# Row sums of two pieces of the exponentials: ScalarE's accumulator or one VectorE instruction, with a new order table

## The chip, the core and the metric

The kernel runs on one core of a Trainium2 chip. The metric is device time in microseconds: the median of three runs of the kernel before is 339.64 us (339.58 to 340.34).

The engines are TensorE (PE: matmuls; PEld are its weight loads), VectorE (DVE), ScalarE (ACT), GpSimd (POOL) and SyncE (SP, which here issues all DMAs). Each has a queue of its own and takes its instructions in order; an instruction whose inputs are not there holds up all that stand behind it on its engine.

## What is computed

Causal attention over 4 batches, 12 heads, 448 tokens and a head size of 64, and then a gated two-layer network with a spatial gate over the tokens:

```python
scores = scale * np.matmul(q, k.transpose(0, 1, 3, 2))
scores = np.where(mask, -1000000000.0, scores)          # mask: above the diagonal
scores = scores - np.max(scores, axis=-1, keepdims=True)
attn = np.exp(scores)
attn = attn / (np.sum(attn, axis=-1, keepdims=True) + 1e-09)
x = np.matmul(attn, v)                                  # then heads side by side: (4, 448, 768)
...
h = gelu(x @ w_in)                                      # 768 -> 1024, tanh form
u, v = (h[..., :d_ff // 2], h[..., d_ff // 2:])
v_n = (v - mu) / np.sqrt(var + 1e-06) * g_ln
v_s = np.einsum('ts,bsd->btd', w_sg, v_n) + b_sg[None, :, None]
return x + (u * v_s) @ w_out                            # 512 -> 768
```

The change touches the exponentials and their row sums.

## The kernel before

The work is cut into 24 pairs of heads (`pair`, six pairs a batch) and four networks (`mlp`, one a batch). No loop sets the order of execution: the functions only enter their steps in a list (`Order.add`, with the engine and with what a step reads and writes), and a table written out by hand, `ORDER`, says in which order the steps are issued. Each engine so gets its steps in the order of the table. A step is one instruction or a few; the table has 1915 of them. Places in a queue, where the text gives them, are counted from 0 in the steps of one engine.

A pair goes this way. SP loads `qk` (448 KB). TensorE makes the scores in two steps (`score`, L433) in four PSUM banks `s`; all PSUM tiles share eight banks. VectorE masks, scales and takes the row minimum of the negative scores in eight steps (`mxs`, L448; each with a read of an accumulator into `ngm`). Only the lower triangle is made; the rows of a head are cut into four chunks (`CH`), and the exponentials of a head into five pieces (`EX`): pieces 0, 2 and 3 have 128 rows and 448, 320 and 128 columns; pieces 1 and 4 have 64 rows and 64 columns. ScalarE makes each piece by one ACTIVATE (L456) into `P`, with an accumulator that adds up the row; its read is a second instruction, ACTIVATION_READ_ACCUMULATOR, which puts the sum in a place of `sm`. The `P` tiles of two heads lie side by side in one tile `PP`, with room for 2 x 1024 columns; there are three such tiles.

From `sm` the step `inv` on VectorE makes the total of each row (L466, TENSOR_REDUCE) and its inverse (L467); it reads all ten places of a pair. TensorE turns the inverses (L470, "the turn"), VectorE copies them (L471), and SP writes them to DRAM (L475) and reads them back spread over the partitions as `rb` (L478). Meanwhile `P` is transposed: for pairs 0 to 7 by TensorE (L500, `tx`, `ty`) and copied to `B` by ScalarE or VectorE (L505, L507), for pairs 8 to 23 by VectorE (L488) and four DMAs. TensorE multiplies with the values (`o`, L526), VectorE multiplies the result with `rb` (L553, `xt`), and `keep_x` splits it in two parts for the network.

The weights are loaded and split in the first 100 us or so beside the pairs: `win` (twelve loads of 512 KB), `wsg` (224 KB each) and `wout` (sixteen of 192 KB), each with a step on ScalarE (L368), two on VectorE (L370, an integer shift, and L372) and two on GpSimd. All matmuls of the networks are at L581; they are issued in steps of three (`group`). Seven matmuls on zeros (L341) stand near the start.

Of the kernel before, what the change touches and what calls it, by code (L numbers as in the profile page):

```python
# [44 lines left out]
PW = 1024  # L45
# [182 lines left out]
def attention_gated_mlp(ctx: ExitStack, tc: tile.TileContext, qk, vP, w_in, g_ln, w_sgT, b_sg, w_out, out):  # L228
# [60 lines left out]
    def act(n, fn, r, w, sb=False, extra=0, ring=()):  # L289
        od.add("act", (0.093 if sb else 0.051) + n / 1200 + 0.093 * extra, fn, r, w, ring=ring)  # L290

    def dve(n, fn, r, w, rate=1.0417, done=0.0, port=False, ring=()):
        od.add("dve", 0.068 + n * rate / 1000, fn, r, w, done, port=port, ring=ring)
# [474 lines left out]
```

## Time and profile before

| | |
|---|---|
| median of three runs | 339.64 us |
| the profiled execution | 341.12 us, of which 339.3 us are the span of the trace |
| TensorE busy | 326.6 us (96%) |
| VectorE busy | 258.3 us (76%) |
| ScalarE busy | 197.2 us (58%) |
| GpSimd busy | 174.1 us (51%) |
| DMA | 57.75 MB, 170 GB/s in the mean |

The profile is one execution. The busy share is a mean over the whole span and hides that the stretches have different limits; so the rows below are of stretches and of single instructions in order of time. In these the number in front is the start in microseconds, the second is the duration; neighbours on one engine overlap a little, so that the time that an instruction holds the queue is read from one start to the next. Idle time ahead of an instruction stands in brackets, with what ended it. "128x448 f32" is partitions by elements.

### The profile page before, as it was taken

To read this page: it belongs to the slowest core of one execution; us is meant where nothing else is said; L and a number is where in the kernel's file an instruction comes from. 1 tells how busy PE (TensorE), PEld (TensorE's weight loads), DVE (VectorE), ACT (ScalarE), POOL (GpSimd) and SP (SyncE) were. 2 spreads that over 40 slices of the span, in tenths; PEclk is the share of its full clock that TensorE was granted. 3 is DMA by queue.
4 is the path that set the end of the run, shared out by engine and by line. 5 is a ranking of instruction groups with operands and counts; after the bars stand their busy time and mean duration, and the time that the engine had idled before them with its cause. 6 is when DMAs were issued, how large, how long until landed. Compare 5 with 4: busy or idle time off the path is not lost.

```text
span 339.3 us, 7630 instructions
## 1 busy us (share of the span) xinstructions
PE 326.6 (96%) x2614; PEld 267.5 (79%) x2615; DVE 258.3 (76%) x762; ACT 197.2 (58%) x658; POOL 174.1 (51%) x225
## 2 busy tenths in 40 slices
PE   3999998999999999999999999999999999999994
PEld 2666675868988878878898878877988988889994
DVE  4899976999999988889699767798877521577512
ACT  3999987996667658476645727384645301344300
POOL 4457666787588843223236608402407833352670
PEclk9999999999999999999999999999999999999998
DMA  7887789592584889857769368557342651201003
GB/s 227 321 251 269 251 247 275 150 322 87 126 228 136 243 218 260 231 143 167 174 187 268 101 208 266 111 155 212 83 115 40 209 141 55 108 2 54 0 29 136
DMA packets 31255, 57.75 MB, mean 170 GB/s; under 512 B 3312, under 2 KB 15344, under 8 KB 31216
## 3 DMA queue, kind: packets, MB, share of 16 engines
q1 hardware_dynamic: 31216, 57.26, 58.1%
q8 instruction: 21, 0.34, 0.4%
q14 instruction: 18, 0.15, 0.2%
HBM read 33.39 MB, written 7.08 MB: 119 GB/s over the span
## 4 chain that ended last, share of the span: by engine, by line
PE 83%; ACT 6%; DVE 4%; DMA 4%; issue 1%; SPq 1%; DVEq 0%; ACTq 0%
PE m L581 63%; PE o L526 10%; PE s L433 8%; ACT P L456 5%; DMA rd<-rT 2%; DVE s L448 1%; DMA g<-in_w_out_dram 1%; DMA qk<-in_qk_dram 1%; ACT B L507 1%; ACT vn L368 1%; PE s L470 1%; DVE vn L372 1%; PE tx L500 1%; PE ty L500 1%; DVE vn L370 0%
## 5 line engine op out<-in xcount | busy, mean ns | idle before, releaser
L456 ACT ACTIVATE P<-s,ngm 64x64 f32<-64x64 f32 (+3 forms) x240 | 100.9, 434 | 35.3 <-DVE ngm L448 28.5
L448 DVE CUSTOM_DVE_ANT_0 s<-s,mask 128x192 f32<-128x192 f32 (+3 forms) x192 | 77.2, 438 | 11.2 <-PE s L433 10.0
L581 PE MATMUL m<-win,x 128*128 128x512 f32 (+1 forms) x264 | 65.7, 399 | 0.1
L581 PE MATMUL m<-x,win 128*128 128x448 f32 x288 | 61.5, 367 | 0.0
L581 PE MATMUL m<-g,wout 128*128 128x448 f32 x288 | 61.3, 368 | 0.0
L581 PEld LDWEIGHTS m<-x,win 128*128 128x128 f32 x288 | 53.7, 188 | 5.2
L581 PEld LDWEIGHTS m<-g,wout 128*128 128x128 f32 x288 | 53.5, 188 | 5.1 <-ACT P L456 0.2
L581 PEld LDWEIGHTS m<-win,x 128*128 128x128 f32 (+1 forms) x264 | 46.7, 183 | 11.9 <-POOL win L375 0.2
L433 PE MATMUL s<-qk 64*64 64x64 f32 (+5 forms) x768 | 46.6, 375 | 6.4 <-DMA qk<-in_qk_dram 5.1
L456 ACT ACTIVATION_READ_ACCUMULATOR P<-s,ngm 128x1 f32 (+1 forms) x240 | 49.9, 208 | 0.0
L433 PEld LDWEIGHTS s<-qk 64*64 64x64 f32 x768 | 30.4, 140 | 23.4 <-issue 10.1
L526 PE MATMUL o<-B,vraw 128*64 128x64 f32 (+4 forms) x672 | 45.3, 291 | 0.3 <-DVE B L505 0.3
L526 PEld LDWEIGHTS o<-B,vraw 128*64 128x64 f32 x672 | 33.0, 137 | 13.5 <-issue 5.5
L488 DVE STREAM_TRANSPOSE P<-P 128x1024 f32<-128x1024 f32 x32 | 38.9, 1228 | 2.1 <-DMA B<-P 1.8
L691 POOL TENSOR_TENSOR res<-x 128x448 f32<-128x448 f32 x24 | 27.6, 1166 | 21.5 <-DMA out_dram<-res 21.3
L581 PE MATMUL m<-wsg,vn 128*128 128x448 f32 x176 | 38.1, 367 | 0.0
L562 POOL TENSOR_TENSOR x<-xt,x 128x448 fp32r<-128x448 f32 x24 | 27.5, 1148 | 15.2 <-ACT x L561 14.9
L581 PEld LDWEIGHTS m<-wsg,vn 128*128 128x128 f32 x176 | 32.7, 188 | 2.9
L704 DVE TENSOR_TENSOR res<-m,res 128x448 f32<-128x448 f32 (+1 forms) x25 | 14.7, 600 | 19.0 <-PE m L581 19.0
L592 ACT ACTIVATE tmp<-tmp 128x448 f32<-128x448 f32 (+2 forms) x32 | 18.9, 601 | 16.4 <-DVE tmp L590 16.4
L625 POOL TENSOR_TENSOR mv<-mv,mhalf 128x1 f32<-128x1 f32 (+1 forms) x16 | 10.0, 626 | 35.8 <-DVE mv L623 35.7
L675 POOL TENSOR_TENSOR tmp<-tmp,g 128x448 f32<-128x448 f32 x16 | 18.3, 1148 | 17.5 <-DVE tmp L671 17.4
(77 smaller groups left out, 395.2 us busy)
## 6 DMA issues: line engine op xcount, KB each, us to landing
B<-P SPq DMA_DIRECT2D x64, 256.0 KB
qk<-in_qk_dram SPq DMA_DIRECT2D x24, 448.0 KB
vn<-in_w_in_dram SPq DMA_DIRECT2D x12, 512.0 KB
vraw<-in_vP_dram SPq DMA_DIRECT2D x24, 256.0 KB
rb<-rd SPq DMA_DIRECT2D x24, 224.0 KB
out_dram<-res SPq DMA_DIRECT2D x9, 448.0 KB
g<-in_w_out_dram SPq DMA_DIRECT2D x16, 192.0 KB
rd<-rT SPq DMA_DIRECT2D x48, 32.0 KB
```

Of the source, the lines that this page charges most:

```text
L433: nc.tensor.matmul(out=s[z][bk].t[64 * h:64 * h + 64, col:col + n], lhsT=qk_.t[r, 0, q0:q0 + 64], rhs=qk_.t[r, 1, k0:k0 + n], start=True, ...
L448: nc.vector.tensor_tensor_reduce(out=o, in0=i, in1=mk, scale=-0.125, scalar=3e38, op0=ALU.add, op1=ALU.min, accum_out=ngm[ib[z]][c][0:m])
L456: act(n, lambda c=c, m=m, k0=k0, n=n, bk=bk, col=col, off=off, kc=kc, i=i, z=z: nc.scalar.activation(out=P[i][0:m, off:off + n], in_=s[z][ ...
L488: dve(PW, lambda z=z: nc.vector.transpose(A[ia][:, :, :, z, :].rearrange("p g t k -> p t g k"), P[ib[z]]), Pk[z] + [kp], Ak, 1.105)
L526: nc.tensor.matmul(out=dst(o.t[r]), lhsT=vr.t[:, c, r], rhs=src(z), start=first and n == 0, stop=last and n == len(lst) - 1)
L562: pool_tt(S, lambda: nc.gpsimd.tensor_tensor(out=y.t[:, S + 64:], in0=x.t, in1=f(y.t)[:, 0:S], op=ALU.subtract), [x, y], [(y, 1)])
L581: nc.tensor.matmul(out=ps.t[0:l().shape[1], 0:n], lhsT=l(), rhs=rr(), start=(k == 0), stop=(k == len(mms) - 1))
L592: act(n, lambda: nc.scalar.activation(out=z(), in_=z(), func=AF.Tanh, scale=GS * GC), [], [t], True)
L625: od.add("pool", 0.46, lambda mv=mv, m=m: nc.gpsimd.tensor_tensor(out=mv.t[0:m, 1:2], in0=mv.t[0:m, 1:2], in1=mhalf[0:m], op=ALU.pow), ["s ...
L675: pool_tt(S, lambda z=z, u=u: nc.gpsimd.tensor_tensor(out=z(), in0=z(), in1=u.t, op=ALU.mult), [u], [t])
L691: pool_tt(S, lambda rr=rr, x=x, k=k: nc.gpsimd.tensor_tensor(out=rr.t[:, k, :], in0=f(x.t)[:, 0:S], in1=f(x.t)[:, S + 64:], op=ALU.add), [ ...
L704: dve(hi - lo, lambda rr=rr, ps=ps, z=z, lo=lo, hi=hi: nc.vector.tensor_tensor(out=rr.t[:, z, lo:hi], in0=ps.t[:, lo:hi], in1=rr.t[:, z, l ...
```

## The change

Pieces 1 and 4 are no longer summed by ScalarE: their ACTIVATE has no accumulator, and its read goes. One VectorE step a pair (`sums`) adds up the rows of these four pieces (two of each head) by one TENSOR_REDUCE over 64 partitions and 2 x 2 rows of 64 elements, and writes the four columns of `sm` that the reads had written. `inv` reads them as before. The table has 24 steps more (1939) and is another one from its start to its end: on TensorE 473 of 551 steps have another place, on VectorE 494 of 538, by up to 61. Nothing else is changed: tiles, buffers, the sizes of loads and what runs on which engine are the same.

```diff
@@ pair
             for z in range(2):
                 i = ib[z]
-                act(n, lambda c=c, ..., i=i, z=z: nc.scalar.activation(
+                own = k not in (1, 4)
+                act(n, lambda c=c, ..., i=i, z=z, own=own: nc.scalar.activation(
                     out=P[i][0:m, off:off + n], in_=s[z][bk].t[0:m, col + k0:col + k0 + n], func=AF.Exp,
-                    bias=ngm[i][c][0:m], scale=-1.0, accum_out=sm[ip][0:m, z, kc[0], kc[1]:kc[1] + 1]),
-                    [s[z][bk], ("ngm", i, c), kp, ks] + ([("P", i, k - 1)] if k == 1 else [("P", i, 2)] if k == 4 else []),
-                    [("P", i, k), ("sm", ip, z, k)], extra=2)
+                    bias=ngm[i][c][0:m], scale=-1.0,
+                    **({"accum_out": sm[ip][0:m, z, kc[0], kc[1]:kc[1] + 1]} if own else {})),
+                    [s[z][bk], ("ngm", i, c), kp] + [ks] * own + ([("P", i, k - 1)] if k == 1 else [("P", i, 2)] if k == 4 else []),
+                    [("P", i, k)] + [("sm", ip, z, k)] * own, extra=2 * own)
+        def sums():
+            t = PP[ib[0] // 2]
+            nc.vector.tensor_reduce(
+                out=sm[ip][0:64].rearrange("p z c t -> p z (c t)")[:, :, 7:10:2][:, :, ::-1],
+                in_=bass.AP(tensor=t.tensor, offset=t.offset + 384, ap=[[2 * PW, 64], [PW, 2], [384, 2], [1, 64]]),
+                op=ALU.add, axis=mybir.AxisListType.X)
+        dve(256, sums, [("P", i, k) for i in ib for k in (1, 4)] + [ks], [("sm", ip, z, k) for z in range(2) for k in (1, 4)])
```

The places that the two tables give to some steps (before, after):

| queue | step | before | after |
|---|---|---|---|
| SP | load of pair 1's `qk` | 2 | 1 |
| SP | load of pair 3's `qk` | 6 | 12 |
| SP | first and second load of `wout` | 17, 32 | 9, 19 |
| ScalarE | the ten exponentials of pair 0 | 1 to 10 | 0 to 10 |
| VectorE | `sums` of pair 0; `inv` of pair 0 | -; 16 | 18; 21 |
| VectorE | `inv` and L553 of pair 3 | 58, 83 | 62, 91 |
| VectorE | `inv` and L553 of pair 5 | 85, 106 | 89, 120 |
| VectorE | `inv` of pair 11 | 245 | 252 |
| TensorE | first scores of pair 3; turn of pair 11 | 22; 189 | 23; 186 |

Up to `inv` of pair 11 the new table has twelve `sums` more on VectorE, and four masks of pair 12 (two of 192 columns, two of 320) and one transpose of pair 11 (L488) less. Up to the turn of pair 11 it has five steps of three output matmuls less on TensorE and two such steps more.

## Rows read from the trace of the kernel before

**Rows 1.** Stretches of the span: microseconds, busy time and instructions of each engine, granted clock, DMA.

```profile
10.00:60.00 50.00, 46.73 (x485) 32.82 (x479) 42.85 (x174) 46.66 (x180) 31.67 (x37) 1.00 0.83 264
10.00:48.70 38.70, 36.73 (x398) 26.51 (x391) 34.32 (x134) 38.67 (x147) 24.00 (x29) 1.00 0.81 263
60.00:118.80 58.80, 58.80 (x477) 48.91 (x476) 57.12 (x168) 43.88 (x142) 47.40 (x64) 1.00 0.63 184
118.80:335.00 216.20, 216.20 (x1617) 182.80 (x1616) 152.58 (x395) 102.38 (x326) 91.02 (x98) 1.00 0.51 142
```

**Rows 2.** Chain that ended last, in order of time: start, microseconds, what.

```profile
15.73 2.39 ACT P L456 x12
...
281.17 53.88 PE m L581 x257
```

**Rows 3.** VectorE in order of time (start, duration, line, shapes), around pair 11's row sums.

```profile
115.05 0.39 DVE L448 CUSTOM_DVE_ANT_0 s<-s,mask 128x192 f32<-128x192 f32 x1
...
115.37 0.52 DVE L448 CUSTOM_DVE_ANT_0 s<-s,mask 128x320 f32<-128x320 f32 x1
...
115.82 0.53 DVE L448 CUSTOM_DVE_ANT_0 s<-s,mask 128x320 f32<-128x320 f32 x1
...
116.27 2.60 DVE L488 STREAM_TRANSPOSE P<-P 128x1024 f32<-128x1024 f32 x2
118.79 0.14 DVE L466 TENSOR_REDUCE tot<-sm 128x8 f32<-128x24 f32 x1
118.96 0.20 DVE L467 RECIPROCAL rs<-tot 128x8 f32<-128x8 f32 x1
```

**Rows 4.** TensorE in order of time: pair 3's scores, pair 8's scores, pair 11's turn.

```profile
20.25 1.16 PE L433 MATMUL s<-qk 64*64 64x448 f32 x12
...
55.84 0.98 PE L433 MATMUL s<-qk 64*64 64x448 f32 x10 [1.23 <-ACT P L456]
...
119.31 0.27 PE L470 MATMUL s<-ident,rs 128*8 128x128 f32 x1
```

**Rows 5.** Groups by line and shape: busy, mean ns of one, idle before.

```profile
L456 ACT ACTIVATION_READ_ACCUMULATOR P<-s,ngm 64x1 f32 x96 | 19.9, 208 | 0.0
...
L448 DVE CUSTOM_DVE_ANT_0 s<-s,mask 128x448 f32<-128x448 f32 x48 | 30.0, 634 | 0.6
...
L448 DVE CUSTOM_DVE_ANT_0 s<-s,mask 64x64 f32<-64x64 f32 x48 | 11.0, 236 | 8.1 <-PE s L433 8.1
...
L466 DVE TENSOR_REDUCE tot<-sm 128x8 f32<-128x24 f32 x24 | 3.9, 164 | 2.1 <-ACT P L456 2.1
```

**Rows 6.** ScalarE in order of time: a 64 by 64 exponential, its read, the next.

```profile
8.78 0.31 ACT L456 ACTIVATE P<-s,ngm 64x64 f32<-64x64 f32 x1
8.97 0.20 ACT L456 ACTIVATION_READ_ACCUMULATOR P<-s,ngm 64x1 f32 x1
9.07 0.31 ACT L456 ACTIVATE P<-s,ngm 64x64 f32<-64x64 f32 x1
```

**Rows 7.** VectorE in order of time: an integer shift of 512 elements.

```profile
8.50 0.41 DVE L370 TENSOR_SCALAR vn<-vn 128x512 int32<-128x512 int32 x1
```

**Rows 8.** VectorE in order of time: seven waits before 60 us, in brackets.

```profile
10.30 0.22 DVE L448 CUSTOM_DVE_ANT_0 s<-s,mask 64x64 f32<-64x64 f32 x1 [0.38 <-PE s L433]
...
11.76 0.37 DVE L448 CUSTOM_DVE_ANT_0 s<-s,mask 128x192 f32<-128x192 f32 x1 [0.26 <-PE s L433]
...
25.45 0.69 DVE L372 SCALAR_TENSOR_TENSOR vn<-vn 128x512 int32<-128x512 int32 x1 [0.57 <-ACT vn L368]
...
39.42 0.62 DVE L553 TENSOR_TENSOR xt<-o,rb 128x448 f32<-128x448 f32 x1 [0.41 <-DMA rb<-rd]
...
45.33 0.43 DVE L370 TENSOR_SCALAR g<-g 128x192 int32<-128x192 int32 x2 [1.38 <-DMA g<-in_w_out_dram]
...
54.12 0.62 DVE L553 TENSOR_TENSOR xt<-o,rb 128x448 f32<-128x448 f32 x1 [1.04 <-DMA rb<-rd]
...
57.01 0.23 DVE L448 CUSTOM_DVE_ANT_0 s<-s,mask 64x64 f32<-64x64 f32 x1 [1.62 <-PE s L433]
```

More of the change, by code (lines that the diff above doesn't have):

```diff
@@ L455, in pair @@
                 i = ib[z]
-                act(n, lambda c=c, m=m, k0=k0, n=n, bk=bk, col=col, off=off, kc=kc, i=i, z=z: nc.scalar.activation(
+                own = k not in (1, 4)
+                act(n, lambda c=c, m=m, k0=k0, n=n, bk=bk, col=col, off=off, kc=kc, i=i, z=z, own=own: nc.scalar.activation(
                     out=P[i][0:m, off:off + n], in_=s[z][bk].t[0:m, col + k0:col + k0 + n], func=AF.Exp,
-                    bias=ngm[i][c][0:m], scale=-1.0, accum_out=sm[ip][0:m, z, kc[0], kc[1]:kc[1] + 1]),
-                    [s[z][bk], ("ngm", i, c), kp, ks] + ([("P", i, k - 1)] if k == 1 else [("P", i, 2)] if k == 4 else []),
-                    [("P", i, k), ("sm", ip, z, k)], extra=2)
+                    bias=ngm[i][c][0:m], scale=-1.0,
[9 more added lines that the diff above has]
+        dve(256, sums, [("P", i, k) for i in ib for k in (1, 4)] + [ks], [("sm", ip, z, k) for z in range(2) for k in (1, 4)])
         sk = [("sm", ip, z, k) for z in range(2) for k in range(5)]
```

185 rows, old and new, of the table ORDER are left out of this document.

## The prediction

> **What bounds the kernel now.** I read the stretches of the span first [rows 1]: what matters is not the share of each engine but where TensorE stops. From 60 us to 335 us it is busy in every microsecond (58.80 of 58.80, then 216.20 of 216.20). Between 10 and 60 us it is busy for 46.73 of 50.00. So time can be won only where TensorE is still waiting for the others, in the first 60 us, or lost where they fall behind it later. The chain that ended last [rows 2] says the same: at first it runs over ScalarE's exponentials, and its last piece is 53.88 us of matmuls without a gap. What holds TensorE up at the start is first ScalarE: from 10 to 48.7 us it is busy 38.67 of 38.70 us [rows 1]. VectorE is next to it: idle 7.15 us between 10 and 60 us and only 1.68 us between 60 and 118.8 us. After 118.8 us VectorE has 63.6 us to spare in 216.2.
>
> The second thing to see is how close VectorE is to TensorE at the end of its dense stretch. Pair 11's row sums are added up (L466) at 118.79 us and inverted at 118.96 us, ready about 119.16 [rows 3]; TensorE turns them at 119.31 us [rows 4]. The slack is 0.15 us, although no wait is shown there. Up to that point the kernel is paced by VectorE's work plus VectorE's idle time: 1.68 + 7.15 = 8.8 us of it idle between 10 us and there. That sum is what I forecast with.
>
> **ScalarE's side: a relief.** Of 240 accumulator reads 96 go, those of the 64 by 64 pieces [rows 5]. The row of one says 208 ns, but a read overlaps its neighbours: an exponential starts at 8.78, its read at 8.97, the next exponential at 9.07 [rows 6]. The read holds the queue for 0.10 us, not 0.21. Four a pair are 0.4 us, the eight pairs that start before 60 us give 3.2 us, and all 24 give 9.6 us, of which those after the first ten pairs lie beside TensorE's unbroken work and are worth nothing. A piece's exponentials are also usable 0.1 us sooner.
>
> **VectorE's side: a load.** One TENSOR_REDUCE a pair over 2 x 2 x 64 = 256 elements of 64 partitions. No row of before has a long one. From the mask rows the slope of one element a partition is (634 - 236) / 384 = 1.04 ns, and the short reduce takes 164 ns for 24 elements, so its base is 139 ns and 256 elements take 404 ns [rows 5]. The next instruction starts about 0.07 us before the end of the one ahead (a mask step of 0.39 us at 115.05, with its read, is followed at 115.37 [rows 3]), so 0.33 us a pair; where L466 stands right behind it and needs its result there is no overlap (118.79, 0.14 long, then 118.96 [rows 3]): 0.44. From below: if it went at the rate of the integer shift (512 elements in 0.41 us [rows 7], less the base 0.53 ns an element), 256 elements would take 0.275 us, 0.21 with the overlap. I take 0.33, because the short reduce and the masks are the nearest rows in kind (one result an element, no doubling seen). In all 24 x 0.33 = 7.9 us; the twelve after pair 11 (4.0 us) are covered by the 63.6 us of idle VectorE, the twelve up to pair 11 (4.0 us) are not covered by anything but idle time.
>
> The Trainium skill has a rule here that speaks against the change. VectorE: DVE Perf Modes, in its rules for kernel authors and its tier table, says that `tensor_reduce` has only a program for one element a cycle, whatever the type, and advises against it on a hot path. By that rule the sum for twelve pairs is 4.0 us; by the shift's row it would be 2.5. No run here shows a long reduce yet.
>
> **The wait it adds.** The new instruction waits for two exponentials of each head, and everything behind it in VectorE's queue waits too, chiefly the next pair's masks, for which ScalarE in turn waits. In the new table the first stands at place 18 of VectorE's queue (counted from 0), behind six masks of pair 1, while the exponentials that it reads end at place 10 of ScalarE's: eleven short steps against seventeen, so ScalarE should be done first. For the later pairs L466 follows within two steps in 16 of 23 cases and within nine in the others, and L466 waited for all ten exponentials already; so I cost the wait at nothing, and if that cover is gone it is the idle time of the first rival.
>
> **The new order.** The table moves most instructions, by up to some 60 places on an engine. On the queues ahead of pair 11's reciprocals I compare what each engine has to do. VectorE: twelve sums more (+4.0), and four masks of pair 12 and one transpose of pair 11 are put behind it: 2 x 0.32 + 2 x 0.45 by their starts (115.05, 115.37, 115.82) and 1.15 of the two transposes' 2.60 [rows 3], so -2.7: net +1.3. TensorE: fifteen matmuls of the last phase go behind the turn and six come ahead of it, nine fewer at 53.88 / 257 = 0.21 us [rows 2]: it comes there 1.8 us sooner. So for the same end VectorE has to be there 1.3 + 1.8 - 0.15 = 3.0 us sooner in waiting: its idle time up to pair 11 has to fall from 8.8 to 5.8 us. What falls below that is gain, microsecond for microsecond, since TensorE runs without a gap behind it.
>
> Seven of these waits make 5.66 us [rows 8]; the rest, all under 0.5 us, I leave as they are. By the table:
> - two on pair 1's scores, 0.64 us: pair 1's load goes from third to second on SP's queue, ahead of 512 KB of weights. Gone.
> - 0.57 on ScalarE's weight step: that step has more room and ScalarE less to do. Gone.
> - 0.41 and 1.04 on the reciprocals that come back from DRAM: from a pair's L467 to its L553 there are 29 steps of VectorE instead of 25 (pair 3) and 31 instead of 21 (pair 5). 1.0 gone.
> - 1.38 on output weights: the first are loaded at places 9 and 19 of SP's queue, not 17 and 32, well ahead of VectorE's use. Gone.
> - 1.62 on pair 8's scores, which themselves waited 1.23 us for a bank that ScalarE's exponentials free [rows 4]: ScalarE has 3.2 us less to do by then. 1.2 gone.
>
> That is 4.8 of 5.66, with nothing new in their place: idle 8.8 - 4.8 = 4.0 us, and a gain of 4.8 - 3.0 = 1.8 us. SP's queue pays for it: pair 3's load stands behind 4992 KB, its own included, not 3328 (by the sizes in the code; six loads are pulled ahead of it), which at the pace of the first stretch (264 GB/s [rows 1]) is there about 19.4 us after the start instead of 12.9; TensorE took it up at 20.25 [rows 4] and does so one group of matmuls later now. One microsecond of margin; I cost it at nothing, else what it overruns. GpSimd's steps follow the weights and have no reader that is late.
>
> **How it stands to the time.** The profiled execution took 341.12 us (339.3 of span), 1.48 above the median of 339.64. 341.12 - 1.8 = 339.3 for such an execution, and 337.8 for the median.
>
> **Rivals.**
> 1. Slower: VectorE becomes the bound up to pair 11. ScalarE's relief is not used, because VectorE, with the sums and the same waits at other places, is late for the masks, and the exponentials wait for them (that ScalarE has to wait for masks soon after 48.7 us, when it is no longer full, speaks for it; that it has no wait of weight before [rows 1] speaks against). If the idle time stays at 8.8 us the price is the whole 3.0 us: 342.6. It decides from 5.8 us of idle up to pair 11.
> 2. No change: between 2.0 and 4.0 us of the waits go, the new load eats them, 338.6 to 340.6, middle 339.6. For it: VectorE is 86% busy in the first of these stretches and 97% in the second, and idle time that is closed at one place opens at another.
> 3. Faster by more: the reduce takes 0.21 us, or every one of the seven waits goes. 12 x 0.12 = 1.4 us gives 336.4; the waits 0.9, 336.9; both 335.5.
> 4. The change doesn't do what it says: the exponential without a read is as long as with it. Then ScalarE gains nothing, its 3.2 us stay, and 1.2 + 0.57 of the waits with it: 339.6, as rival 2.
>
> **How the numbers follow.** The forecast has 0.48 (336.9 to 338.6: gains of 2.7 to 1.0 us), rival 3 0.10, rivals 2 and 4 together 0.26, rival 1 0.16. A run of this kernel can tell some 0.3%, 1.0 us, from no change, so faster is below 338.6: 0.48 + 0.10 = 0.58; same 0.26; slower, above 340.7: 0.16. The range leaves out the far half of rival 3 and most of rival 1: 336.0 to 340.9.
>
> **What would show it.** Right: no read between 64 by 64 exponentials and starts 0.19 us apart; reduces of 64 x 256 of about 0.40 us; VectorE idle about 4 us between 10 us and pair 11's L466, and that row about 1.2 to 3.6 us earlier than 118.79, at the same or a little more VectorE work; TensorE without a gap behind it. Wrong: TensorE idle after 60 us, or waits of VectorE on `P` at the new line (the wait is real); a reduce of 0.28 us (rival 3); a late `qk` of pair 3 near 20 us; waits of TensorE on VectorE between 65 and 125 us (rival 1).

## The result, and the profile after

The changed kernel takes 342.88 us (median of four runs, 342.74 to 343.09), the kernel before beside it 339.99 (339.58 to 340.83). The ratio is 1.0082, with a 95% interval of 1.0060 to 1.0105: slower by 0.8%, where 337.8 us, a gain of 0.5%, was forecast. The profiled execution took 342.94 us with a span of 341.2, against 341.12 and 339.3 before; that execution of before had already lost 0.9 us at its start (last section), so by the profiles the loss is 1.8 us, and by the medians 2.9.

The stretches of the changed kernel (microseconds, then busy time and instructions of TensorE, its weight loads, VectorE, ScalarE and GpSimd, granted clock, DMA):

```profile
10.00:60.00 50.00, 44.67 (x484) 31.05 (x485) 46.47 (x185) 48.42 (x163) 31.63 (x38) 1.00 0.81 269
60.00:115.95 55.95, 55.95 (x437) 45.57 (x436) 53.64 (x156) 38.64 (x114) 43.28 (x61) 1.00 0.70 196
60.00:118.80 58.80, 58.80 (x451) 48.08 (x450) 56.49 (x167) 38.86 (x114) 46.13 (x64) 1.00 0.67 187
118.80:335.00 216.20, 215.10 (x1608) 181.05 (x1607) 157.56 (x402) 97.66 (x281) 91.83 (x99) 1.00 0.49 138
```

Against [rows 1] VectorE's idle time falls as hoped, from 7.15 to 3.53 us in the first stretch. But TensorE's does not: it stands 5.33 us instead of 3.27 between 10 and 60 us, and after 118.8 us it has a hole of 1.10 us where it had none. The first of these two differences is no measure of the loss: the slow scores at the start of that execution of before count as busy (last section), and a version further down that is as fast as the kernel before stands 5.23 us in the same window. The start of a single step, TensorE's turn of pair 11, tells more.

VectorE around pair 11's row sums, which answers to [rows 3] (L466 is now the sum, L476 and L477 are the old L466 and L467):

```profile
114.74 0.39 DVE L466 TENSOR_REDUCE sm<-P 64x4 f32<-64x256 f32 x1
115.73 0.18 DVE L476 TENSOR_REDUCE tot<-sm 128x8 f32<-128x24 f32 x1 [0.60 <-ACT P L458]
115.95 0.20 DVE L477 RECIPROCAL rs<-tot 128x8 f32<-128x8 f32 x1
```

TensorE's turn of pair 11, which answers to [rows 4], and its last phase:

```profile
117.53 0.27 PE L480 MATMUL s<-ident,rs 128*8 128x128 f32 x1
...
313.78 0.78 PE L591 MATMUL m<-x,win 128*128 128x448 f32 x3
315.61 6.74 PE L591 MATMUL m<-wsg,vn 128*128 128x448 f32 x32 [1.05 <-DVE vn L648]
322.19 15.14 PE L591 MATMUL m<-g,wout 128*128 128x448 f32 x72
```

The reciprocals are ready at 116.15 us, and TensorE comes for them at 117.53, 1.4 us later; before, the slack was 0.15 us [rows 3, 4]. VectorE has become 3.0 us earlier (118.96 to 115.95), TensorE only 1.8 (119.31 to 117.53). Those 1.8 are the nine matmuls that were moved behind the turn: at pair 11 nothing is won. Something is lost there, in fact. In an execution of the old order without the slow start (the experiment with the two adds moved, below) the turn comes at 118.41 us:

```profile
118.41 0.27 PE L473 MATMUL s<-ident,rs 128*8 128x128 f32 x1
```

Less the 1.8 us of moved matmuls that is 116.6, and the changed kernel is 0.9 us behind it. The loss has two places. The first is on ScalarE at the start. First the order before, then the changed one (the row x4 merges three exponentials of 64 by 64 and the next one, of 128 by 448):

```profile
0.72 1.28 ACT L368 ACT_TABLE_LOAD   x1 [0.72 <-PEq L757]
7.00 0.67 ACT L368 ACTIVATE vn<-vn 128x512 f32<-128x512 f32 x1 [5.00 <-DMA vn<-in_w_in_dram]
7.56 0.62 ACT L456 ACTIVATE P<-s,ngm 128x448 f32<-128x448 f32 x1
```

```profile
7.17 1.28 ACT L458 ACT_TABLE_LOAD   x1 [7.17 <-DVE ngm L449]
8.47 0.63 ACT L458 ACTIVATE P<-s,ngm 128x448 f32<-128x448 f32 x1
...
12.29 1.24 ACT L458 ACTIVATE P<-s,ngm 64x64 f32<-64x64 f32 x4
```

ScalarE's function table is loaded ahead of its first activation. Before, the first one was a weight step: the load stood at 0.72 us, and its 1.28 us passed while the weights were still on their way. In the new order the first one is an exponential, which waits for VectorE's first masks; the load starts only when that wait is over, at 7.17 us, and the first exponential at 8.47 instead of 7.56. Why the load ran ahead of the wait in the one case and behind it in the other, no row shows. The Trainium skill gives the load about 1283 ns (ScalarE: Activation LUTs, What ACT_TABLE_LOAD costs), and the row agrees.

The second place is the tail. In the layer norm of the last network VectorE scales its last chunk, in two tiles, by the inverse deviations that GpSimd makes (L637). Its two steps and GpSimd's steps beside them, in the changed kernel, by engine:

```profile
308.92 0.55 DVE L637 TENSOR_SCALAR tmp<-tmp,mv 128x512 f32<-128x512 f32 x1 [0.73 <-POOL mv L635]
310.45 3.72 DVE L637 TENSOR_SCALAR tmp<-tmp,mv 64x512 f32<-64x512 f32 x1 [0.72 <-POOL mv L635]
```

```profile
309.87 0.54 POOL L635 TENSOR_TENSOR mv<-mv,mhalf 64x1 f32<-64x1 f32 x1 [0.99 <-DVE mv L633]
310.39 1.29 POOL L643 TENSOR_TENSOR vn<-tmp,vn 128x512 fp32r<-128x512 f32 x1
311.64 2.25 POOL L701 TENSOR_TENSOR res<-x 128x448 f32<-128x448 f32 x2
```

The smaller tile takes 3.72 us, the larger one just ahead of it 0.55. It starts 0.06 us after the start of three GpSimd steps that follow each other without a pause (the last two, L701, are residual adds) and ends at 314.17, 0.28 us after the last of them (313.89). The chain L637, `vn`, L591 is what TensorE then waits 1.05 us for. In the order before the scaling of the smaller tile stood alone (last row). The stretching was to be seen in that trace all the same, at a place where TensorE did not wait for it: beside a single residual add (first row) a tile of 128 rows took 1.37 us (second row) and ended 0.29 us after the add.

```profile
303.61 1.15 POOL L691 TENSOR_TENSOR res<-x 128x448 f32<-128x448 f32 x1
303.68 1.37 DVE L627 TENSOR_SCALAR tmp<-tmp,mv 128x512 f32<-128x512 f32 x1 [0.81 <-POOL mv L625]
...
311.35 0.54 DVE L627 TENSOR_SCALAR tmp<-tmp,mv 64x512 f32<-64x512 f32 x1 [0.19 <-POOL mv L625]
```

### The profile page after: what moved, and what is told of

Read it like the earlier page. It is cut to its first block, busy times and chain, and to the rows that moved or that the text cites. A ratio compares the mean times of both kernels' runs of the same rounds, so it can differ in the third digit from the quotient of the medians.

```text
span 341.2 us, 7547 instructions
## 1 busy us (share of the span) xinstructions
PE 326.7 (96%) x2614; PEld 265.8 (78%) x2615; DVE 266.7 (78%) x786; ACT 187.7 (55%) x562; POOL 173.5 (51%) x225
## 4 chain that ended last, share of the span: by engine, by line
PE 76%; ACT 10%; DVE 6%; issue 3%; POOL 2%; DMA 1%; DVEq 0%; POOLq 0%; ACTq 0%
PE m L591 53%; PE o L536 11%; PE s L434 10%; ACT P L458 5%; DVE tmp L637 2%; ACT B L517 2%; PE ty L510 1%; DVE s L449 1%; DMA qk<-in_qk_dram 1%; ACT vn L369 1%; PE tx L510 1%; DVE tmp L600 1%; POOL tmp L685 1%; POOL g L688 1%; POOL mv L635 1%
## 5 line engine op out<-in xcount | busy, mean ns | idle before, releaser
L458 ACT ACTIVATE P<-s,ngm 64x64 f32<-64x64 f32 (+3 forms) x240 | 95.8, 436 | 35.0 <-DVE ngm L449 32.3
L449 DVE CUSTOM_DVE_ANT_0 s<-s,mask 128x192 f32<-128x192 f32 (+3 forms) x192 | 76.4, 440 | 7.0 <-PE s L434 6.4
L591 PE MATMUL m<-win,x 128*128 128x512 f32 (+1 forms) x264 | 64.2, 396 | 0.0
L591 PE MATMUL m<-g,wout 128*128 128x448 f32 x288 | 62.2, 370 | 0.0
L591 PE MATMUL m<-x,win 128*128 128x448 f32 x288 | 61.1, 368 | 0.0
L591 PEld LDWEIGHTS m<-g,wout 128*128 128x128 f32 x288 | 53.3, 188 | 5.9 <-POOL g L688 0.6
L591 PEld LDWEIGHTS m<-x,win 128*128 128x128 f32 x288 | 53.7, 188 | 5.4
L591 PEld LDWEIGHTS m<-win,x 128*128 128x128 f32 (+1 forms) x264 | 47.3, 183 | 11.6
L434 PE MATMUL s<-qk 64*64 64x64 f32 (+5 forms) x768 | 45.0, 372 | 5.9 <-DMA qk<-in_qk_dram 4.0
L591 PE MATMUL m<-wsg,vn 128*128 128x448 f32 x176 | 38.8, 370 | 1.0 <-DVE vn L648 1.0
L591 PEld LDWEIGHTS m<-wsg,vn 128*128 128x128 f32 x176 | 32.4, 188 | 4.7 <-DVE vn L648 1.4
L701 POOL TENSOR_TENSOR res<-x 128x448 f32<-128x448 f32 x24 | 27.7, 1171 | 7.7 <-DMA out_dram<-res 7.6
L599 ACT ACTIVATE tmp<-m 128x448 f32<-128x448 f32 (+1 forms) x28 | 15.7, 564 | 27.1 <-PE m L591 25.3
L458 ACT ACTIVATION_READ_ACCUMULATOR P<-s,ngm 128x1 f32 x144 | 30.3, 210 | 0.0
```

The source lines that it names most:

```text
L434: nc.tensor.matmul(out=s[z][bk].t[64 * h:64 * h + 64, col:col + n], lhsT=qk_.t[r, 0, q0:q0 + 64], rhs=qk_.t[r, 1, k0:k0 + n], start=True, ...
L449: nc.vector.tensor_tensor_reduce(out=o, in0=i, in1=mk, scale=-0.125, scalar=3e38, op0=ALU.add, op1=ALU.min, accum_out=ngm[ib[z]][c][0:m])
L458: act(n, lambda c=c, m=m, k0=k0, n=n, bk=bk, col=col, off=off, kc=kc, i=i, z=z, own=own: nc.scalar.activation(out=P[i][0:m, off:off + n], ...
L591: nc.tensor.matmul(out=ps.t[0:l().shape[1], 0:n], lhsT=l(), rhs=rr(), start=(k == 0), stop=(k == len(mms) - 1))
L599: act(n, lambda: nc.scalar.activation(out=z(), in_=h(), func=AF.Square), [ps], [t])
L701: pool_tt(S, lambda rr=rr, x=x, k=k: nc.gpsimd.tensor_tensor(out=rr.t[:, k, :], in0=f(x.t)[:, 0:S], in1=f(x.t)[:, S + 64:], op=ALU.add), [ ...
```

## The experiments

All ratios are to the kernel before, run beside. Where an edit only reorders steps, the diff shows the queue concerned.

**The change in the old order.** The table of before, with each pair's sum right ahead of its `inv`.

```diff
 VectorE, table of before, every pair p:
+    sums of pair p
     inv of pair p
```

> The change with the old table: each pair's sum stands directly ahead of its L466 (this kernel's L476), nothing else moves. Theory (the slowdown comes from two places of the new table and not from the sums): VectorE pays 12 x 0.33 to 0.44 = 4.0 to 5.3 us up to pair 11, where the old table had 0.15 us of slack; ScalarE's 3.2 us give back part of its waits; so 340.5 to 342, slower than 339.99 but with TensorE without a gap after 300 us. Rival (the sums themselves make the kernel slow): 343 or more. Second rival (ScalarE's relief is worth more than the load): 339 or less.

Measured: 341.91 us (341.29 to 343.65), ratio 1.0067 (1.0042 to 1.0092). TensorE's waits for VectorE after 60 us, where the kernel before has none:

```profile
91.57 0.27 PE L483 MATMUL s<-ident,rs 128*8 128x128 f32 x1 [0.29 <-DVE rs L480]
110.63 1.18 PE L437 MATMUL s<-qk 64*64 64x320 f32 x20 [0.18 <-DVE tmp L684]
119.07 0.27 PE L483 MATMUL s<-ident,rs 128*8 128x128 f32 x1 [0.38 <-DVE rs L480]
```

In the old order VectorE does become the later engine: the sums are there, the slack of 0.15 us at pair 11 is gone, and the time is within the 340.5 to 342 expected. The three waits make 0.85 us, and the profiled execution (341.29 us) is the fastest of the seven; where the rest of the median's 1.9 us lies is not shown. ScalarE, full from 10 to 48.7 us before, is busy 36.92 of 38.70 there, and stands before masks (six waits, 4.1 us up to 60 us, against three and 3.2):

```profile
ACT P L461 <- DVE ngm L452: 4.1, 6, 2.1
```

**The table alone.** The kernel before, accumulators and all, in the new order less the sums.

```diff
-ORDER = (table of before)
+ORDER = (table after, without its 24 sums)
```

> The new table with the old instructions: ScalarE's accumulators add up all five pieces, and there is no sum on VectorE. Theory: the late activation table load near 7 us and the gap of TensorE near 315 us belong to the table, so both are still there, and the time is 341.5 to 343.5. Rival (the sums make the kernel slow): 340 or less.

Measured: 345.45 us (345.00 to 345.74), ratio 1.0158 (1.0132 to 1.0183). That is above the 341.5 to 343.5 expected. The new order by itself costs 5.4 us, and in it the sums gain 2.6 (345.45 to 342.88). So the sums are not what makes the changed kernel slow; the order is.

**The function table first.** The changed kernel; a small activation that is in the program anyway goes to the head of ScalarE's queue.

```diff
-    84, 128, 1, 2, 0, 4, 85, ...
+    84, 128, 1, 3, 2, 0, 4, 85, ...
```

> The changed kernel with one step of its table moved: the small activation that is there to load ScalarE's function table comes first in ScalarE's queue, not late. Theory (the load of 1.28 us, which now stands behind the first mask's wait, starts ScalarE late in a stretch in which it is never idle): the first exponential at 7.2 us, not 8.47; pair 7's turn 0.8 to 1.3 us earlier than 60.01; 341.6 to 342.2. Rival (VectorE paces the start, ScalarE has the time): 342.9, no change, and pair 7's turn at 60.

Measured: 342.11 us (341.47 to 342.37), ratio 1.0054 (1.0029 to 1.0078). The two intervals overlap, but TensorE's turns come 0.8 to 1.1 us earlier than in the changed kernel, from the first pair to the last; the hole in the tail stays (1.07 us).

**Two adds out of the way.** The changed kernel; GpSimd's two residual adds stand ahead of the last chunk's inverse deviations (and one output DMA with them).

```diff
-    ... 1480, 1475, 1751, ..., 1788, 1812, ..., 1805, 1476, 1896, 1895, 1834, ...
+    ... 1480, 1475, 1476, 1751, ..., 1788, 1896, 1895, 1812, ..., 1805, 1834, ...
```

> The changed kernel with three steps of its table moved: two GpSimd residual adds of the last batch (L701) come ahead of the third chunk's inverse deviation, not behind it, and the output DMA that frees their buffer comes earlier on SP's queue. Theory (VectorE's L637 of the last chunk, 3.72 us long at 310.45, is held by GpSimd's three instructions of 1.15 to 1.29 us beside it; TensorE waits for it): L637 takes 0.55 us, TensorE has no gap of 1.05 us near 315, 341.0 to 341.6. Rival (the last batch's first phase is late by the order of its matmuls, and L637 is slow for another reason): 342.5 to 343, gap still there.

Measured: 341.35 us (341.17 to 341.84), ratio 1.0031 (1.0013 to 1.0048). The scaling takes 1.51 us, since one GpSimd step still lies beside it (it ends 0.28 us after that step), and the hole is gone.

```profile
311.00 1.29 POOL L646 TENSOR_TENSOR vn<-tmp,vn 128x512 fp32r<-128x512 f32 x1
311.06 1.51 DVE L640 TENSOR_SCALAR tmp<-tmp,mv 64x512 f32<-64x512 f32 x1 [0.72 <-POOL mv L638]
```


**Both moves.**

```diff
 both diffs above
```

> The changed kernel with both moves at once: the small activation that loads ScalarE's function table stands first in ScalarE's queue, and GpSimd's two residual adds stand ahead of the first of the last chunk's inverse deviations. If the two losses are separate (one at the start, one in the tail), their gains add: 342.9 - 0.8 - 1.5 = 340.6 us, no gap of TensorE before the last chunk's first matmuls with wsg, and TensorE's turns some 0.8 us earlier than in the changed kernel all the way. Rival: the start's gain is used up by a later wait on VectorE, as it is in the kernel with the old table, and the time stays at 341.3. It would be a surprise below 340.0, the time of the kernel before, since VectorE still has 24 sums of 0.33 us more and ScalarE only 96 readings of 0.10 us less.

Measured: 340.26 us (339.96 to 340.85), ratio 0.9992 (0.9979 to 1.0005). The two losses are separate and add, as far as the intervals can tell; together they are the whole of the changed kernel's loss. What is left is a kernel that can't be told from the one before.

```profile
10.00:60.00 50.00, 44.77 (x488) 32.32 (x489) 47.09 (x187) 48.41 (x164) 32.02 (x38) 1.00 0.80 270
60.00:115.13 55.13, 55.13 (x431) 44.78 (x430) 53.14 (x154) 37.89 (x111) 42.92 (x60) 1.00 0.71 199
118.80:335.00 216.20, 216.14 (x1614) 182.36 (x1612) 155.80 (x401) 97.33 (x280) 91.48 (x98) 1.00 0.50 140
```

These are its stretches; the second ends at pair 11's reciprocals. VectorE is idle 4.90 us up to there. By the forecast's own rule (what falls below 5.8 is gain) it should have gained 0.9 us, a ratio of 0.9974, which lies just outside the interval.

**The collision brought into the kernel before.** Two residual adds moved right behind the last chunk's last inverse deviation; one of them stood earlier before, the other later.

```diff
 GpSimd, table of before:
     inverse deviation of the last chunk's last piece (L625)
+    residual add, residual add (L691)
```

> The kernel before, with two of GpSimd's residual adds moved right behind the last chunk's last inverse deviation, where the new table has its own; nothing else moved. If the long scaling step on VectorE in the tail of the changed kernel (3.72 us instead of 0.55) comes from GpSimd's adds running beside it, the same scaling step of the kernel before grows from 0.54 to about 3 us or more, TensorE waits some 1 us before the last chunk's first matmuls with wsg, and the time is 341 to 342 us. Rival: the long step has another cause (the sums, or the order of VectorE); then the step stays at 0.55 us and the time at 340.0.

Measured: 340.74 us (340.23 to 342.00), ratio 1.0013 (1.0001 to 1.0026). The step on VectorE and the adds on GpSimd:

```profile
309.74 2.47 DVE L630 TENSOR_SCALAR tmp<-tmp,mv 64x512 f32<-64x512 f32 x1 [0.19 <-POOL mv L628]
```

```profile
309.68 2.25 POOL L694 TENSOR_TENSOR res<-x 128x448 f32<-128x448 f32 x2
```

The long step is shown to come from GpSimd's adds: 2.47 us instead of 0.54, again 0.28 us longer than the run beside it, with no sums and in the old order. Its price is smaller than expected (0.4 us, hardly clear of noise, not 1 to 2): TensorE does not wait at any place after 60 us here, since the old order leaves it other work. The stretching and the loss are two things. The Trainium skill (SBUF — State Buffer, SBUF: two separate sides) says that GpSimd and a VectorE instruction in one of its two-port modes share a pair of memory ports, which whoever starts first keeps for the whole instruction while the other blocks. These rows agree, though none shows which mode the scaling ran in, and they show more: the scaling lasts until 0.28 us after the whole run of GpSimd steps, and not only after the one that was ahead of it.

**Sums for the first six pairs alone, in the old order.**

```diff
-                own = k not in (1, 4)
+                own = p >= 6 or k not in (1, 4)
...
-        dve(256, sums, ...)
+        if p < 6:
+            dve(256, sums, ...)
```

> The kernel before in its old order, with the sums on VectorE for pairs 0 to 5 alone; the pairs from 6 on keep ScalarE's accumulator. If the old order loses because VectorE becomes late after about 50 us (pairs 6 and later, when ScalarE has slack and VectorE none), the relief of ScalarE in the first stretch stays, up to 1.8 us at TensorE's turn of pair 6, and VectorE has 18 sums fewer: 339 to 340.3 us. Rival: what is gained early is lost to VectorE whatever the later pairs do, since VectorE is the later engine by pair 11 in any case: 340 to 341.9.

Measured: 341.04 us (339.98 to 342.96), ratio 1.0013 (0.9991 to 1.0035): no gain. ScalarE is busy 36.80 of 38.70 us from 10 to 48.7 where it was full before, so most of the 2.4 us of relief turned into idle time there, and TensorE waits 1.4 us for reciprocals before 60 us (0.5 before). This is the rival's side of the expectation.

**Sums for the first six pairs, new order, both moves.** The same diff on the kernel with both moves.

> The changed kernel with both moves (table load first, two residual adds earlier) and the sums on VectorE for pairs 0 to 5 alone. If VectorE's 18 later sums are a loss to the end, 1 us or more below the one with both moves and all sums: 339 to 340. Rival: the new order was made with the sums of all pairs in it, and with the accumulators back ScalarE is late again in it (the new order without any sums was 2.6 us slower than with them): 341 or more.

Measured: 340.57 us (340.27 to 341.27), ratio 1.0008 (0.9997 to 1.0019). Eighteen sums fewer on VectorE and 72 reads more on ScalarE change nothing that can be measured. Both theories missed: after pair 5 neither side of the exchange has a price in this order that shows.

**Each sum of pairs 0 to 11 twice.** On the kernel with both moves.

```diff
-            nc.vector.tensor_reduce(
+            for _ in range(2 if p < 12 else 1):
+              nc.vector.tensor_reduce(
```

> The kernel with both moves (340.26 us), but each of the sums of pairs 0 to 11 is issued twice, so that VectorE has 12 more steps of 0.33 us, 4.0 us, up to pair 11's reciprocals; nothing else is changed. If VectorE's work plus the idle time that it can't close sets the pace up to pair 11, most of the 4.0 us shows in the time: 342.5 to 344.3, with VectorE's idle time from 10 us to pair 11 about what it was (4.9 us). Rival: the idle time left there is time in which VectorE merely waits for a ScalarE that is the bound, so that it takes the sums up: the idle time falls by 2 us or more and the time rises by under 2 us, to 340.5 to 342.2.

Measured: 340.63 us (340.12 to 341.08), ratio 1.0008 (0.9997 to 1.0018): 0.4 us more by the medians for 4.0 us of VectorE, and the intervals of the two kernels overlap. VectorE around pair 11:

```profile
115.40 0.82 DVE L470 TENSOR_REDUCE sm<-P 64x4 f32<-64x256 f32 x2
116.32 0.18 DVE L480 TENSOR_REDUCE tot<-sm 128x8 f32<-128x24 f32 x1
116.53 0.20 DVE L481 RECIPROCAL rs<-tot 128x8 f32<-128x8 f32 x1
```

The reciprocals come 1.4 us later (115.13 to 116.53), since 1.5 us of the idle time close (4.90 to 3.41) and the other steps' busy time shows 1.1 us less; TensorE's turn follows at 116.88 instead of 116.72. The slack has shrunk from 1.4 to 0.15 us, so hardly more VectorE work would fit in (an estimate from these rows; no run tries it). The time is the rival's, though the idle time fell by less than the 2 us it named: in the new order VectorE does not set the pace up to pair 11.

**The new start in the old order,** without sums, and **with sums for six pairs.**

```diff
 SP:       load of pair 0's qk
+          load of pair 1's qk
           first weight block
-          load of pair 1's qk
 ScalarE: +small activation (function table)
-          weight step
           four exponentials of pair 0
+          weight step
 VectorE:  the two steps of that weight block one and two places later
```

> The kernel before with the start of the new order alone: pair 1's load second in SP's queue, ScalarE's first weight step behind the first four exponentials, and the small activation that loads the function table at the head of ScalarE's queue; no sums. The first exponential then starts at about 7.1 us instead of 7.6 to 8.1, and pair 1's scores follow pair 0's without the wait of 1.2 to 1.6 us. If the 0.5 to 0.9 us that ScalarE gains at its start reach the end, 339.4 to 339.8; if VectorE, which had 0.15 us of slack at pair 11, takes them back, 340.0 to 340.6.

> The same start in the old order, with the sums on VectorE for pairs 0 to 5. By the one theory (up to 50 us ScalarE sets the pace, and what it gains is kept) the start's gain and the relief of 6 x 0.40 us add up to 338 to 339.5; by the other (VectorE takes it all back by pair 11, as it did without the new start) 340 to 341.5.

Measured: 340.33 us (340.08 to 343.48), ratio 1.0017 (0.9999 to 1.0036), and 340.98 us (339.97 to 341.37), ratio 1.0010 (0.9998 to 1.0022). Neither gains. In the second ScalarE again stands before masks, 4.2 us between its first exponential and 60 us. No version tried beats the kernel before.

**Both moves, no sums.** The new order as in the kernel of 340.26 us, with ScalarE's accumulators for all.

```diff
-ORDER = (table of before)
+ORDER = (table after with both moves, without its 24 sums)
```

> The new order with both moves, as in the kernel of 340.26 us, but with no sums at all: ScalarE's accumulators give all row sums, as in the kernel before. By the theory that the sums pay where ScalarE is full (10 to 30 us) and cost next to nothing on VectorE, this is slower than the same order with all sums by what the relief is worth, 2.1 us at pair 7 by the two runs without the moves: 342.4 to 342.9, and 2 us or more above the one with sums for six pairs alone (340.57). Rival: in the repaired order ScalarE is no longer the bound, and the sums are worth nothing either way: 340.0 to 341.

Measured: 342.48 us (342.17 to 343.14), ratio 1.0051 (1.0033 to 1.0069). As the first theory expected: the sums are worth about 2 us in this order too (2.2 by the medians), and with the run of six pairs all of that lies in the first six. ScalarE is full from 10 to 30 us (the fourth busy time of the row, 20.00 of 20.00), so four reads a pair more make it later:

```profile
10.00:30.00 20.00, 16.12 (x168) 10.65 (x169) 17.35 (x68) 20.00 (x82) 10.06 (x11) 1.00 0.83 283
```

TensorE's turn of pair 5, in the kernel with both moves and then without the sums:

```profile
44.13 0.27 PE L483 MATMUL s<-ident,rs 128*8 128x128 f32 x1
```

```profile
45.85 0.27 PE L473 MATMUL s<-ident,rs 128*8 128x128 f32 x1
```

The lag of 1.7 us is there by pair 5, and at pair 11 it is 1.8 (116.72 and 118.49). The new order without sums is still 0.5% behind the old one when both losses are mended. Where that lies was not isolated.

## Why the prediction was wrong, step by step

- **The read, 0.10 us each, and ScalarE's relief: right.** In the changed kernel three exponentials of 64 by 64 start at 12.29, 12.49 and 12.68 us and the next one, of 128 by 448, at 12.88: 0.19 to 0.20 us apart, with no read between. ScalarE's busy time falls from 197.2 to 187.7 us (9.6 forecast). In the new order the relief is worth 2.2 to 2.6 us, against 3.2 assumed up to 60 us; in the old order no run gains by it.
- **The sum, 0.33 us: right.** The group of the 24 sums in the changed kernel, mean 405 ns (404 forecast):

```profile
L466 DVE TENSOR_REDUCE sm<-P 64x4 f32<-64x256 f32 x24 | 9.7, 405 | 3.6 <-ACT P L458 3.4
```

 The next instruction starts 0.34 us after a sum (13.12, 13.46). So the slope of [rows 5] holds, and the shift's rate [rows 7] does not. The Trainium skill's rule that `tensor_reduce` has only the program for one element a cycle (VectorE: DVE Perf Modes, the tier table) agrees with that.
- **The wait of the sum, costed at nothing: nearly.** VectorE waits 3.4 us for ScalarE ahead of sums in the whole run, but 0.75 us before 60 us.
- **VectorE's work: 1.3 us more forecast, none found.** From 10 us to pair 11's reciprocals it is 100.11 us against 100.10. The queue differs by exactly the steps named; eleven of the integer shifts were 0.8 us shorter in sum, and the rest was not traced. `inv` at 115.73 us, 3.06 us earlier, lies within the 1.2 to 3.6 forecast.
- **The first step that failed: "with nothing new in their place".** All seven waits of [rows 8] are gone, more than was forecast. But new ones came: 0.89 us on the first weight step at 10.76 us, which is due to the late function table (it is not there when the table is loaded first); 0.58 on scores, 0.54 and 0.21 ahead of sums before 60 us; 0.78 ahead of L481 at 60.32 us; 0.61 and 0.60 shortly before pair 11's L476. The idle time up to pair 11's reciprocals is 3.53 + 2.31 = 5.84 us, not 4.0. By the forecast's own rule (what falls below 5.8 is gain) this alone takes the whole 1.8 us away and leaves no change.
- **The second step that failed: "What falls below that is gain, microsecond for microsecond, since TensorE runs without a gap behind it."** VectorE was in time, even with 1.4 us to spare, since the 1.3 us of work more did not come. But being in time earlier is no gain. TensorE runs without a gap *ahead* of the turn as well (55.95 of 55.95 us from 60 us on), and so it comes there when its own work lets it. The sums issued twice show it: 4.0 us of VectorE cost 0.4. The gain could be made only before 60 us, where TensorE stands, as the first paragraph of the prediction said; and there the changed kernel loses 0.9 us. The account should have been kept by when TensorE comes to a step, not by VectorE's idle time.
- **"TensorE runs without a gap behind it" failed again in the tail,** and with it "GpSimd's steps follow the weights and have no reader that is late". GpSimd's two residual adds, at their new place, made VectorE late for the last chunk. Moving them out of the way gives 0.5% (ratio 1.0082 to 1.0031).
- **A cost that was not seen: the function table.** The table of places showed that ScalarE's first step is now an exponential; that the load of 1.28 us goes with the first step was in the trace of before and was not read. Moving it gives 0.3% (1.0082 to 1.0054).
- **The first rival has the time, but by luck.** Its mechanism, VectorE late for masks and reciprocals, is what the change does in the old order (ratio 1.0067). In the new one the time is near its 342.6, 342.88, by other causes.
- **Pair 3's load, one microsecond of margin: right.** No wait on it in the changed kernel: TensorE's only wait for a load is the very first.

Together: the order costs 5.4 us, of which some 3 are the two losses that were mended and the rest is open; the sums give 2.6 back; the difference of 2.8 is the 2.9 us measured, within what the medians scatter.

## What to carry to other kernels

Keep the account on the engine whose end is the kernel's end: time that a feeder gains in front of an engine that is already dense only becomes slack. When an order is made anew, look at what the first and the last few steps of each queue now wait for, table loads included, and at which long steps on GpSimd now lie beside VectorE's. And try the change and the order apart: here the same change gained about 2 us in the new order and lost about 2 in the old one, and the new order cost more than the change gained in it.

## What the runs showed of the hardware beyond that

In the old order's executions the first 32 scores take 3.26 or 3.27 us wherever a row shows them alone. The second group of 32 took 3.27 us in the profiled execution of the kernel before and 1.76 in that with the adds moved, whose order is the same up to there; the granted clock is 1.00 (the 2.4 GHz level) in both, and TensorE had stood still for 1.25 us ahead of the slower and 1.57 us ahead of the faster one. First the former, then the latter:

```profile
8.41 3.27 PE L433 MATMUL s<-qk 64*64 64x448 f32 x32 [1.25 <-DMA qk<-in_qk_dram]
```

```profile
8.63 1.76 PE L436 MATMUL s<-qk 64*64 64x448 f32 x32 [1.57 <-DMA qk<-in_qk_dram]
```

The first pair's turn comes at 13.72 and 12.84 us in these two, and pair 11's at 119.31 and 118.41, the same 0.9 us apart. Two other versions in the old order have one of each: 1.76 us behind a wait of 0.63 (the change in the old order) and 3.27 behind 1.11 (the sums of six pairs). So the length of the wait does not decide it, and what does is open. It may be a part of why runs of the kernel before scatter from 339.4 to 342.6 us, while four of the changed one lie within 0.4 us; that is not shown. The execution that the prediction was read from is one with the slow start.
